# Constants out of the PSUM bank of the states, a conversion with one hand-over, normalization spread over each phase, and weights spilled in order of use

## The chip, the cores and the metric

One core of a Trainium2 chip runs the whole program. The metric is the device time of one execution in microseconds; lower is better. The engines are named as the profile names them: PE is TensorE (matmuls), PEld its weight loads, DVE VectorE, ACT ScalarE, POOL GpSimd, SP the queue that issues most DMAs.

## The reference

Three layers follow one another. Batch is 4, the sequence 768, the model width 384 (8 heads of 48).

```python
# 1. gated linear attention, per head, state 48x48, y goes on as x (4, 768, 384)
state = alpha[:, :, t, :, None] * state + einsum('bhd,bhe->bhde', k[:, :, t], v[:, :, t])
y[:, :, t] = einsum('bhd,bhde->bhe', q[:, :, t], state)
# 2. gated MLP
h = gelu_tanh(x @ w_in)                    # w_in 384 x 1024
u, v = h[..., :512], h[..., 512:]
v_n = (v - mean(v)) / sqrt(var(v) + 1e-6) * g_ln
v_s = einsum('ts,bsd->btd', w_sg, v_n) + b_sg[None, :, None]   # w_sg 768 x 768
x = x + (u * v_s) @ w_out                  # w_out 512 x 384
# 3. Fourier mixing and channel MLP
u = x + real(fft(fft(x, axis=1), axis=2))
out = u + relu(layernorm(u) @ w_ch1) @ w_ch2                   # 384 x 1536 x 384
```

## The kernel before

All three layers are in one program and overlap only at their seams; each engine executes its instructions in the order in which the code writes them. Precise products are made of three matmuls on a high and a low part (`mm3`, L425 to L427).

**Attention.** The 32 heads are taken as 16 groups of two heads; a group `g` is done in two "halves" `h` of three 128-column chunks each. One pass of the loop over `h` writes: for the group two ahead, on even halves `scan1` (L105, a scan along the sequence, then a tiny maximum and a reciprocal) and on odd halves `khat` (L118), `scan2` (L114) and, on POOL, `qhat` (L127); on even halves also `zscan` (L150), which sums the state contributions; then the scores `sc` of half `h+1` and their masking `att` (L163, tile `at`); two `fill` calls, which hand out one step each of the weight conversion below; `pv` (L171 to L177), and `kv` of the next group (L145, L146). `kv` writes the 288 columns of `kp`, a view of a whole PSUM bank `full`. In the same bank lie four constants, one column each: `one` and `tiny`, which the scans and the maximum read, and two bit masks, which the conversion reads. So whoever reads a constant and whoever writes `kp` are ordered one behind the other.

**Weight conversion.** The weights come as 64-bit floats and are put together as 32-bit floats by class `Wide`, in 62 jobs of 128 rows by 256 or 192 columns: 12 for `win` (w_in), 8 for `wo` (w_out) and 42 "spill" jobs for w_ch1 and w_ch2, which go back to DRAM for the last layer. A job takes two steps. `first`: a bit mask on DVE (L444 with the mask in PSUM, in the attention; L442 with an immediate, afterwards), then three ACT instructions (`mid`, `low`, and a relu on `x`). `second`: a sum on POOL (L464), an or on DVE (L465), a second bit mask on DVE (L444 or L442), then on POOL a product (L467) and a sum (L468). A job then ends with a split into high and low parts (ACT, and POOL L399) or with a DMA. The `fill` calls of the attention take steps until the 12 `win` jobs and 6 spill jobs are done: 19 jobs have both steps behind them by half 20, one in each half from half 2.

**Gated MLP** (`gmlp`). Per batch row `b` there are six `v` units and eight `u` units (matmuls and a gelu each, `vunit` and `uunit`), the normalization `norm(b)` of `v` (13 tiny DVE instructions, then for each of six tiles L684 and, on DVE after a copy on ACT, L687 into `vl`), and `spatial(b)`: 8 rounds `d` of 18 matmuls with `vl`, `vh` and `wsg`, a gating chain on DVE and ACT, and the output product `wout` with `wo`. The row order is: early units, the last eight of `us(1)`, `spatial(0)`, `vs(2) + us(2)` (14 units), `spatial(1)`, `vs(3)` (6 units), `spatial(2)`, `us(3)` (8 units), `spatial(3)` together with the Fourier mixing. `proj` runs a phase of units and hands out the normalization for the spatial stage that follows, one step a unit, two in the last `n` units, and what is left behind the last unit. `gfill` hands out conversion steps, `3 + d % 2` a round in `spatial` and `c` a unit in `proj`.

The scan is listed in the order of instructions below as SCALAR_TENSOR_TENSOR and in the profile as TENSOR_TENSOR_SCAN.

## Time and profile before

| what | value |
|---|---|
| median of 3 runs | 830.95 us (826.39, 830.95, 830.97) |
| profiled execution, its own time | 830.67 us |
| its span in the profile | 828.9 us |
| mean granted clock of PE, share of full speed | 0.951 |
| PE, PEld busy | 766.2 us (92%), 707.7 us (85%) |
| DVE, ACT, POOL busy | 509.8 us (61%), 321.3 us (39%), 260.7 us (31%) |

The span is cut by the work on PE: attention 0 to 205.5 us, `us(1)` to 218.0, `spatial(0)` to 273, `vs(2) + us(2)` to 305, `spatial(1)` to 345.7, `vs(3)` to 359.5, `spatial(2)` to 404.4, `us(3)` to 418.5, `spatial(3)` with the mixing to 477, and the channel MLP to the end. The share of busy time is a mean over these stages; a stage is read by which engine has no gaps in it, and by what ended the gaps of the others. The profile's view of the chain that ended last is empty here, so the reading goes by stretches, waits and timelines. In a timeline row the bracket is the time that the engine sat idle before the instruction, and what released it.

### The profile page before, as it was taken

What the parts mean: (1) busy time and instruction counts of PE and PEld (TensorE: products, weight loads), DVE (VectorE), ACT (ScalarE), POOL (GpSimd) and SP (SyncE); (2) the same over time, 40 slices, a digit from 0 to 9 for tenths busy, and PEclk for the clock granted to TensorE, in tenths of its full rate; (3) what the DMA queues carried; (4) which work ended last, traced back from release to release, by engine and by line L of the source; (5) the groups of instructions that cost most, each with busy time, mean ns of one, the idle gap of its engine ahead of it and who ended that gap; (6) DMA issues with size and microseconds to landing.
All of it is one profiled execution on the core that took longest, in us unless ns stands there. A gap on an engine that the chain in (4) does not pass through costs nothing.

```text
span 828.9 us, 13575 instructions
## 1 busy us (share of the span) xinstructions
PE 766.2 (92%) x5077; PEld 707.7 (85%) x5077; DVE 509.8 (61%) x1166; ACT 321.3 (39%) x757; POOL 260.7 (31%) x309
## 2 busy tenths in 40 slices
PE   7688888999779979879999999999999999999996
PEld 5476667777769779859999989999999999999996
DVE  6787688774578888896657767336643354424321
ACT  3555656653554464442233345123222222122210
POOL 2366765430467666634023276102000000000000
PEclk9755898999989999989999999999999999999999
DMA  9978576723412333320012033000000000000001
GB/s 231 195 172 167 125 163 159 169 59 75 122 52 77 105 93 98 90 62 30 1 42 77 1 87 105 29 1 29 2 29 2 30 1 1 30 1 28 11 19 33
DMA packets 43596, 58.07 MB, mean 70 GB/s; under 512 B 5472, under 2 KB 34176, under 8 KB 43520
## 3 DMA queue, kind: packets, MB, share of 16 engines
q1 hardware_dynamic: 42944, 56.85, 27.2%
q8 instruction: 42, 0.69, 0.3%
q10 hardware_dynamic: 576, 0.26, 0.1%
q14 instruction: 34, 0.28, 0.1%
HBM read 42.93 MB, written 9.44 MB: 63 GB/s over the span
## 4 chain that ended last, share of the span: by engine, by line


## 5 line engine op out<-in xcount | busy, mean ns | idle before, releaser
L1031 DVE SCALAR_TENSOR_TENSOR hl<-h,hh 128x384 fp32r<-128x384 f32 x96 | 53.4, 556 | 143.4 <-ACT hh L1030 143.4
L1030 ACT ACTIVATE hh<-h 128x384 fp32r<-128x384 f32 x96 | 47.2, 492 | 178.0 <-PE h L427 178.0
L425 PE MATMUL h<-unh,wc 128*128 128x384 f32 x288 | 99.3, 345 | 0.0
L426 PE MATMUL h<-unl,wc 128*128 128x384 f32 x288 | 96.5, 335 | 0.1
L427 PE MATMUL a<-wc,hl 128*128 128x384 f32 x288 | 96.4, 335 | 0.0
L427 PE MATMUL h<-unh,wc 128*128 128x384 f32 x288 | 96.3, 334 | 0.0
L426 PE MATMUL a<-wc,hh 128*128 128x384 f32 x288 | 96.2, 334 | 0.0
L425 PE MATMUL a<-wc,hh 128*128 128x384 f32 x288 | 96.2, 334 | 0.0
L427 PE MATMUL h<-wsg,vl 128*128 128x384 f32 x192 | 67.3, 351 | 5.8 <-DVE vl L687 5.8
L426 PE MATMUL h<-wsg,vh 128*128 128x384 f32 x192 | 67.3, 351 | 4.4 <-POOL wsg L399 4.4
L425 PE MATMUL h<-wsg,vh 128*128 128x384 f32 x192 | 67.0, 349 | 0.0
L467 POOL TENSOR_TENSOR wm<-wm,wr 128x192 f32<-128x192 f32 (+1 forms) x62 | 45.3, 731 | 47.1 <-DVE wr L442 29.6
L426 PEld LDWEIGHTS h<-unl,wc 128*128 128x128 f32 x288 | 54.2, 188 | 0.3 <-DVE unl L399 0.3
L427 PEld LDWEIGHTS a<-wc,hl 128*128 128x128 f32 x288 | 54.1, 188 | 0.2 <-DVE hl L1031 0.2
L425 PEld LDWEIGHTS h<-unh,wc 128*128 128x128 f32 x288 | 54.1, 188 | 0.0
L425 PEld LDWEIGHTS a<-wc,hh 128*128 128x128 f32 x288 | 54.1, 188 | 0.0
L427 PEld LDWEIGHTS h<-unh,wc 128*128 128x128 f32 x288 | 54.1, 188 | 0.0
L426 PEld LDWEIGHTS a<-wc,hh 128*128 128x128 f32 x288 | 54.1, 188 | 0.0
L464 POOL TENSOR_TENSOR wm<-wm,wr 128x192 f32<-128x192 f32 (+1 forms) x62 | 47.1, 759 | 20.8 <-ACT wr L459 20.6
L468 POOL TENSOR_TENSOR wm<-wx,wm 128x192 f32<-128x192 f32 (+1 forms) x62 | 48.6, 784 | 4.9
L465 DVE SCALAR_TENSOR_TENSOR wx<-wr,wx 128x192 int32<-128x192 int32 (+1 forms) x62 | 29.2, 472 | 29.3 <-ACT wx L460 29.3
L460 ACT ACTIVATE wx<-wx,bias 128x192 int32<-128x192 int32 (+1 forms) x62 | 29.8, 480 | 43.1 <-DVE wx L442 27.4
(217 smaller groups left out, 1951.5 us busy)
## 6 DMA issues: line engine op xcount, KB each, us to landing
ak<-in_qa SPq DMA_DIRECT2D x26, 290.4 KB, 4.8
v<-in_v SPq DMA_DIRECT2D x16, 288.0 KB, 4.2
wr<-in_w_d SPq DMA_DIRECT2D x18, 256.0 KB, 2.7
wr<-in_w_d SPq DMA_DIRECT2D x24, 192.0 KB, 2.4
raw<-w_s SPq DMA_DIRECT2D x12, 384.0 KB, 3.3
out<-o SPq DMA_DIRECT2D x24, 192.0 KB, 1.9
...
```

Of the source, the lines that this page charges most:

```text
L425: T.matmul(out, lh, rh, start=first, stop=False)
L426: T.matmul(out, lh, rl, start=False, stop=False)
L427: T.matmul(out, ll, rh, start=False, stop=last)
L460: nc.scalar.activation(x, x, AF.Relu, scale=8.0, bias=self.const)
L464: nc.gpsimd.tensor_tensor(out=mid, in0=mid, in1=j["low"], op=ALU.add)
L465: nc.vector.scalar_tensor_tensor(out=x, in0=hi, scalar=-2 ** 31, in1=x, op0=ALU.bitwise_and, op1=ALU.bitwise_or)
L467: nc.gpsimd.tensor_tensor(out=mid, in0=mid, in1=hi.bitcast(F32), op=ALU.mult)
L468: nc.gpsimd.tensor_tensor(out=mid, in0=x.bitcast(F32), in1=mid, op=ALU.add)
L1030: A.activation(hh, p, AF.Relu)
L1031: V.scalar_tensor_tensor(out=hl, in0=p, scalar=0.0, in1=hh.bitcast(F32), op0=ALU.max, op1=ALU.subtract)
```

## The change

- The four constants leave the PSUM bank: `kp` is a tile of its own columns, `one` an SBUF tile, `tiny` and the masks immediates. The multiplier `pb` of `zscan` becomes two fixed tiles, and ACT writes five of six columns of it.
- The conversion in the attention (`on_dve`): `first` is a bit mask on DVE (L446), the relu on ACT, and a `scalar_tensor_tensor` on DVE (L450) for `mid` and `low` together; `second` is the or (L460), the second mask (L461) and the product (L463) on DVE, and one sum on POOL (L466). After the attention the old form stays.
- The jobs run `win`, `wo`, spill, with the spill in the order in which the last layer uses it; the attention takes steps only until the 12 `win` jobs are done, 13 jobs by half 14.
- `gfill` hands out 4 steps a round instead of `3 + d % 2`. `proj` spreads the seven steps of `norm` evenly over the units. The phases around `spatial(2)` are `vs(3)` and four units of `us(3)` before it, and the other four after it.
- The pool of the conversion lies on the other side of the memory, and what is left of it is drained after `gmlp`.

```diff
-    full = ps_t.tile([128, 512], F32, name="kp")
-    bank, masks = full[0:R2], [full[:, D * NC + 2 + i:D * NC + 3 + i].bitcast(I32) for i in range(2)]
-    kp, one, tiny = bank[:, 0:D * NC].rearrange("p (e c) -> p e c", c=NC), bank[:, D * NC:D * NC + 1], bank[:, D * NC + 1:D * NC + 2]
+    kp = ps_t.tile([R2, D, NC], F32, name="kp")
+    one = const("one", [R2, 1])
+    pbs = [const(f"pb{i}", [R2, D, NC]) for i in range(2)]
...
-        V.tensor_tensor(out=p0, in0=sf[:, cs, 0], in1=tiny.to_broadcast(list(p0.shape)), op=ALU.max)
+        V.tensor_scalar(out=p0, in0=sf[:, cs, 0], scalar1=1e-14, scalar2=None, op0=ALU.max)
...
-            G[g]["pb"] = w_p.tile([R2, D, NC], F32, tag="pb", name="pb")
-            A.copy(G[g]["pb"], sfs[g % 3][:, None, :, 0].to_broadcast([R2, D, NC]))
+            A.copy(pbs[g % 2][:, :, 1:], sfs[g % 3][:, None, 1:, 0].to_broadcast([R2, D, NC - 1]))
...
-        self.mask(x, j["hi"], 0)
-        nc.scalar.activation(mid, h16[:, :, 2], AF.Copy, scale=2.0 ** -20)
-        nc.scalar.activation(low, h16[:, :, 1], AF.Copy, scale=2.0 ** -36)
-        nc.scalar.activation(x, x, AF.Relu, scale=8.0, bias=self.const)
+        nc.vector.tensor_scalar(out=x, in0=j["hi"], scalar1=0x7FFF0000, scalar2=None, op0=ALU.bitwise_and)
+        j["on_dve"] = self.on_dve
+        if self.on_dve:
+            nc.scalar.activation(x, x, AF.Relu, scale=8.0, bias=self.const)
+            nc.vector.scalar_tensor_tensor(out=mid, in0=h16[:, :, 2], scalar=65536.0, in1=h16[:, :, 1], op0=ALU.mult, op1=ALU.add)
+        else:
...
-        nc.gpsimd.tensor_tensor(out=mid, in0=mid, in1=j["low"], op=ALU.add)
+        if not j["on_dve"]:
+            nc.gpsimd.tensor_tensor(out=mid, in0=mid, in1=j["low"], op=ALU.add)
         nc.vector.scalar_tensor_tensor(out=x, in0=hi, scalar=-2 ** 31, in1=x, op0=ALU.bitwise_and, op1=ALU.bitwise_or)
-        self.mask(hi, x, 1)
-        nc.gpsimd.tensor_tensor(out=mid, in0=mid, in1=hi.bitcast(F32), op=ALU.mult)
+        nc.vector.tensor_scalar(out=hi, in0=x, scalar1=-2 ** 23, scalar2=None, op0=ALU.bitwise_and)
+        if j["on_dve"]:
+            nc.vector.scalar_tensor_tensor(out=mid, in0=mid, scalar=2.0 ** -36, in1=hi.bitcast(F32), op0=ALU.mult, op1=ALU.mult)
+        else:
+            nc.gpsimd.tensor_tensor(out=mid, in0=mid, in1=hi.bitcast(F32), op=ALU.mult)
         nc.gpsimd.tensor_tensor(out=mid, in0=x.bitcast(F32), in1=mid, op=ALU.add)
...
+    for q in range(KF // 2):
+        for i in range(KD):
+            c = slice(q * 256, q * 256 + 256)
+            js.append((rows(st["w1_d"], i, c, True), 256, put("w1_s", i, c)))
+        for i in (2 * q, 2 * q + 1):
+            for c in (slice(0, 192), slice(192, 384)):
+                js.append((rows(st["w2_d"], i, c, True), 192, put("w2_s", i, c)))
...
-    def proj(units, b, n, c):
-        ns = norm(b)
+    def proj(units, b, c):
+        ns, n = norm(b), NT + 1
...
-            take(ns, 1 + (i >= len(units) - n))
+            take(ns, n * (i + 1) // len(units) - n * i // len(units))
...
-                st["gfill"](h, 3 + d % 2)
+                st["gfill"](h, 4 if b < B - 1 else 2)
...
-    proj(vs(3), 2, 1, 1)
+    proj(vs(3) + us(3)[0:KH], 2, 1)
     spatial(2)
-    proj(us(3), 3, 0, 1)
+    proj(us(3)[KH:], 3, 0)
...
-    wide = wd.steps(first + spill[0:6] + second + spill[6:])
+    wide = wd.steps(first + second + spill)
...
-    front(lambda n, h: take(wide, n) if wd.n_done < len(first) + 6 else None, F["wsg"])
+    front(lambda n, h: take(wide, n) if wd.n_done < len(first) else None, F["wsg"])
     ready(len(first))
-    st["wo_ready"] = lambda d: ready(len(first) + 6 + len(second) * (d + 1) // KH)
+    st["wo_ready"] = lambda d: ready(len(first) + len(second) * (d + 1) // KH)
```

On DVE in the attention, from one masking of the scores to the next, this stands in a row before (`sf`, `ak`, `qh` are the tiles of the scans, `wr` the raw weights, `wx` and `wm` the parts of a job):

```order
L163 TENSOR_TENSOR at<-sp,mask 128x768
L444 TENSOR_TENSOR wx<-wr,kp 128x256
L465 SCALAR_TENSOR_TENSOR wx<-wr,wx 128x256
L444 TENSOR_TENSOR wr<-wx,kp 128x256
L150 SCALAR_TENSOR_TENSOR z<-kp,pb 112x288
L105 SCALAR_TENSOR_TENSOR sf_121<-ak_115,kp 112x779
L106 MEMSET ak_115 112x6
L108 TENSOR_TENSOR p_825<-sf_121,kp 112x6
L109 RECIPROCAL ak_115<-p_825 112x6
L163 TENSOR_TENSOR at<-sp,mask 128x768
L444 TENSOR_TENSOR wx<-wr,kp 128x256
```

And now, from the same masking:

```order
L162 TENSOR_TENSOR at<-sp,mask 128x768
L446 TENSOR_SCALAR wx<-wr 128x256
L450 SCALAR_TENSOR_TENSOR wm<-wr 128x256
L460 SCALAR_TENSOR_TENSOR wx<-wr,wx 128x256
L461 TENSOR_SCALAR wr<-wx 128x256
L463 SCALAR_TENSOR_TENSOR wm<-wm,wr 128x256
L149 SCALAR_TENSOR_TENSOR z<-kp,pb_129 112x288
L105 SCALAR_TENSOR_TENSOR sf_121<-ak_115,one 112x779
L106 MEMSET ak_115 112x6
L108 TENSOR_SCALAR p_805<-sf_121 112x6
L109 RECIPROCAL ak_115<-p_805 112x6
L162 TENSOR_TENSOR at<-sp,mask 128x768
```

Each job has five instructions on DVE in place of three, none reads `kp`, and the scan of L105 reads `one`.

On PE, at the states of one half (a name behind "waits" is the engine or queue whose semaphore is waited for), before:

```order
L172 MATMUL y<-at,v 48x128
L171 MATMUL y<-at,v 64x128
L172 MATMUL y<-at,v 48x128
L177 MATMUL y<-qh_124,z 48x128 x6
L145 MATMUL kp<-v,kt 64x48 [waits DVE_49,Activation_49]
L146 MATMUL kp<-v,kt 48x48
L145 MATMUL kp<-v,kt 64x48
L146 MATMUL kp<-v,kt 48x48
```

And now:

```order
L171 MATMUL y<-at,v 48x128
L170 MATMUL y<-at,v 64x128
L171 MATMUL y<-at,v 48x128
L176 MATMUL y<-qh_124,z 48x128 x6
L144 MATMUL kp<-v,kt 64x48 [waits Activation_49]
L145 MATMUL kp<-v,kt 48x48
L144 MATMUL kp<-v,kt 64x48
L145 MATMUL kp<-v,kt 48x48
```

The wait of the first `kp` matmul for DVE is gone; the one for ACT, which copies `kt`, stays.

On DVE at the end of the phase ahead of `spatial(2)`, where `vt` and `vl` are the tiles of the normalization and `bs` the statistics of the next row, before:

```order
L617 BN_STATS bs_92<-vt_87 128x6
L618 BN_AGGR mv_90<-bs_92 128x2
L684 TENSOR_SCALAR vt_86<-vt_86,mv_89,gy 128x512
L687 TENSOR_TENSOR vl<-vt_86,vh 128x512
L442 TENSOR_SCALAR wx<-wr 128x192
L617 BN_STATS bs_91<-vt_87 128x6
L618 BN_AGGR mv_90<-bs_91 128x2
L684 TENSOR_SCALAR vt_86<-vt_86,mv_89,gy 128x512
L687 TENSOR_TENSOR vl<-vt_86,vh 128x512 x2
L465 SCALAR_TENSOR_TENSOR wx<-wr,wx 128x192
L442 TENSOR_SCALAR wr<-wx 128x192
L617 BN_STATS bs_92<-vt_87 128x6
```

And now:

```order
L446 TENSOR_SCALAR wx<-wr 128x256
L683 TENSOR_SCALAR vt_86<-vt_86,mv_89,gy 128x512
L686 TENSOR_TENSOR vl<-vt_86,vh 128x512
L460 SCALAR_TENSOR_TENSOR wx<-wr,wx 128x256
L461 TENSOR_SCALAR wr<-wx 128x256
L683 TENSOR_SCALAR vt_86<-vt_86,mv_89,gy 128x512
L686 TENSOR_TENSOR vl<-vt_86,vh 128x512
L446 TENSOR_SCALAR wx<-wr 128x256
L686 TENSOR_TENSOR vl<-vt_86,vh 128x512
L460 SCALAR_TENSOR_TENSOR wx<-wr,wx 128x256
L461 TENSOR_SCALAR wr<-wx 128x256
```

Before, the statistics of the last `v` unit stand behind the last `vl`; now three `vl` stand behind all statistics, among the conversion steps of the four `u` units (L683 and L686 are L684 and L687 of before).

## Rows read from the trace of the kernel before

**Rows 1.** Busy time of each engine in three stretches (times in us).
```profile
core 0: us, PE busy (x) PEld busy (x) DVE busy (x) ACT busy (x) POOL busy (x), PEclk, DMA share, GB/s
33.00:111.00 78.00, 64.39 (x571) 49.49 (x572) 59.99 (x95) 46.74 (x117) 53.19 (x58) 0.68 0.75 163
150.00:200.00 50.00, 48.95 (x547) 39.54 (x546) 33.40 (x49) 27.22 (x62) 16.00 (x13) 1.00 0.41 91
360.00:404.50 44.50, 38.72 (x206) 37.24 (x205) 29.76 (x63) 13.74 (x33) 15.38 (x23) 0.92 0.10 30
```
**Rows 2.** Waits by pair of lines: total us, times, longest us.
```profile
PE kp L145 <- DVE wr L444: 7.9, 7, 2.5
DVE z L150 <- PE kp L146: 17.0, 10, 4.2
PE h L427 <- DVE vl L687: 5.8, 4, 2.0
```
**Rows 3.** Timeline of DVE, first scan of the third group: start, us, instruction, idle before.
```profile
24.95 1.78 DVE L105 TENSOR_TENSOR_SCAN sf<-ak,kp 112x779 f32<-112x779 f32 x1 [3.29 <-PE kp L146]
```
**Rows 4.** Timeline of DVE, one pair of halves with conversion work.
```profile
44.71 0.92 DVE L163 TENSOR_TENSOR at<-sp,mask 128x768 f32<-128x768 f32 x1
...
46.52 0.43 DVE L465 SCALAR_TENSOR_TENSOR wx<-wr,wx 128x256 int32<-128x256 int32 x1 [0.57 <-ACT wx L460]
46.98 0.42 DVE L444 TENSOR_TENSOR wr<-wx,kp 128x256 int32<-128x256 int32 x1
47.32 1.08 DVE L118 TENSOR_TENSOR sf<-ak,sf 112x768 f32<-112x768 f32 x1
...
54.33 0.76 DVE L150 TENSOR_TENSOR_SCAN z<-kp,pb 112x288 f32<-112x288 f32 x1 [0.84 <-PE kp L146]
55.00 1.75 DVE L105 TENSOR_TENSOR_SCAN sf<-ak,kp 112x779 f32<-112x779 f32 x1
...
57.10 0.92 DVE L163 TENSOR_TENSOR at<-sp,mask 128x768 f32<-128x768 f32 x1
```
**Rows 5.** Timeline of DVE, the masking of the scores at four points.
```profile
32.33 0.92 DVE L163 TENSOR_TENSOR at<-sp,mask 128x768 f32<-128x768 f32 x1
...
116.92 0.93 DVE L163 TENSOR_TENSOR at<-sp,mask 128x768 f32<-128x768 f32 x1
...
154.76 0.93 DVE L163 TENSOR_TENSOR at<-sp,mask 128x768 f32<-128x768 f32 x1
...
199.65 0.92 DVE L163 TENSOR_TENSOR at<-sp,mask 128x768 f32<-128x768 f32 x1
```
**Rows 6.** Timeline of DVE, one mask instruction at two points.
```profile
306.18 0.67 DVE L442 TENSOR_SCALAR wx<-wr 128x192 int32<-128x192 int32 x1
...
310.92 0.26 DVE L442 TENSOR_SCALAR wx<-wr 128x192 int32<-128x192 int32 x1
```
**Rows 7.** Timeline of POOL: a split, `qhat`, and the sum beside 306.18.
```profile
46.86 0.73 POOL L399 TENSOR_TENSOR win<-wm,win 128x256 fp32r<-128x256 f32 x1 [3.27 <-ACT win L396]
...
103.63 1.70 POOL L127 TENSOR_TENSOR qh<-q,qh 112x768 f32<-112x768 f32 x1
...
306.10 0.62 POOL L464 TENSOR_TENSOR wm<-wm,wr 128x192 f32<-128x192 f32 x1
```
**Rows 8.** Timeline of DVE, a conversion instruction beside the POOL instruction at 103.63.
```profile
104.72 2.27 DVE L465 SCALAR_TENSOR_TENSOR wx<-wr,wx 128x256 int32<-128x256 int32 x1 [0.57 <-ACT wx L460]
```
**Rows 9.** Timeline of PE, a wait in `spatial(0)` and one in the 14-unit phase.
```profile
233.86 0.44 PE L425 MATMUL a<-gh,wo 128*128 128x384 f32 x1 [2.20 <-ACT wo L396]
...
292.20 0.44 PE L425 MATMUL h<-xh,win 128*128 128x384 f32 x1 [1.88 <-ACT vt L614]
```
**Rows 10.** Timeline of DVE in `spatial(1)`: first of four conversion steps, and the work behind them.
```profile
326.30 0.25 DVE L442 TENSOR_SCALAR wx<-wr 128x192 int32<-128x192 int32 x1
...
329.37 0.60 DVE L719 SCALAR_TENSOR_TENSOR t<-h,gt,bb 128x384 f32<-128x384 f32 x1
```
**Rows 11.** Timeline of DVE, the last `vl` before `spatial(2)` and before `spatial(3)`.
```profile
368.40 0.68 DVE L687 TENSOR_TENSOR vl<-vt,vh 128x512 fp32r<-128x512 f32 x1
...
416.58 0.69 DVE L687 TENSOR_TENSOR vl<-vt,vh 128x512 fp32r<-128x512 f32 x1 [0.87 <-ACT vh L685]
```

More of the change, by code (lines that the diff above doesn't have):

```diff
@@ L149, in zscan @@
         z = G[g]["z"] = w_p.tile([R2, D, NC], F32, tag="z", name="z")
-        V.tensor_tensor_scan(out=flat(z), data0=flat(kp), data1=flat(G[g]["pb"]), initial=0.0, op0=ALU.add, op1=ALU.mult)
+        V.tensor_tensor_scan(out=flat(z), data0=flat(kp), data1=flat(pbs[g % 2]), initial=0.0, op0=ALU.add, op1=ALU.mult)
     def sc(h, i):
@@ L220, in attention @@
     V.memset(one, 1.0)
-    V.memset(tiny, 1e-14)
-    for m, z in zip(masks, Wide.MASKS):
-        V.memset(m, z)
-    st["wide"].masks = masks
+    for p in pbs:
+        V.memset(p[:, :, 0], 0.0)
     warmup(4)
@@ L304, in attention @@
             flag(tc, st, ones[:, 0:2], w_p, ps_t)
-    st["wide"].masks = None
+    st["wide"].on_dve = False
     ctx.close()
@@ L430 @@
 class Wide:
-    MASKS = 0x7FFF0000, -2 ** 23
     def __init__(self, nc, pool, w, const, ahead):
         self.nc, self.pool, self.w, self.const, self.ahead = nc, pool, w, const, ahead
-        self.n_done, self.masks = 0, None
+        self.n_done, self.on_dve = 0, True
     def tile(self, n, dt, w, bufs):
         return self.pool.tile([128, self.w], dt, tag=n, name=n, bufs=bufs)[:, 0:w]
-    def mask(self, out, x, i):
-        if self.masks is None:
-            self.nc.vector.tensor_scalar(out=out, in0=x, scalar1=self.MASKS[i], scalar2=None, op0=ALU.bitwise_and)
-        else:
-            self.nc.vector.tensor_tensor(out=out, in0=x, in1=self.masks[i].to_broadcast(list(x.shape)), op=ALU.bitwise_and)
     def load(self, job):
@@ L456, in first @@
         low = j["low"] = j["raw"].bitcast(F32).rearrange("p (a b) -> p a b", b=2)[:, :, 0]
[L457 to L460 removed]
+        nc.vector.tensor_scalar(out=x, in0=j["hi"], scalar1=0x7FFF0000, scalar2=None, op0=ALU.bitwise_and)
[4 more added lines that the diff above has]
+        else:
+            nc.scalar.activation(mid, h16[:, :, 2], AF.Copy, scale=2.0 ** -20)
+            nc.scalar.activation(low, h16[:, :, 1], AF.Copy, scale=2.0 ** -36)
+            nc.scalar.activation(x, x, AF.Relu, scale=8.0, bias=self.const)
     def second(self, j):
         nc, x, mid, hi = self.nc, j["x"], j["mid"], j["hi"]
[L464 removed]
+        if not j["on_dve"]:
+            nc.gpsimd.tensor_tensor(out=mid, in0=mid, in1=j["low"], op=ALU.add)
         nc.vector.scalar_tensor_tensor(out=x, in0=hi, scalar=-2 ** 31, in1=x, op0=ALU.bitwise_and, op1=ALU.bitwise_or)
[L466 to L467 removed]
+        nc.vector.tensor_scalar(out=hi, in0=x, scalar1=-2 ** 23, scalar2=None, op0=ALU.bitwise_and)
[3 more added lines that the diff above has]
+            nc.gpsimd.tensor_tensor(out=mid, in0=mid, in1=hi.bitcast(F32), op=ALU.mult)
         nc.gpsimd.tensor_tensor(out=mid, in0=x.bitcast(F32), in1=mid, op=ALU.add)
@@ L551, in spill_jobs @@
     js = []
-    for n, d, rr, cc in (("w1_s", "w1_d", KD, FF), ("w2_s", "w2_d", KF, DM)):
-        for i in range(rr):
-            w = WJ if cc % WJ == 0 else 192
-            for c in range(0, cc, w):
-                c = slice(c, c + w)
-                js.append((rows(st[d], i, c, True), w, put(n, i, c)))
+    for q in range(KF // 2):
[5 more added lines that the diff above has]
+                js.append((rows(st["w2_d"], i, c, True), 192, put("w2_s", i, c)))
     return js
@@ L695, in proj @@
                 flush()
-            take(ns, 1 + (i >= len(units) - n))
+            take(ns, n * (i + 1) // len(units) - n * i // len(units))
             st["gfill"](-1, c)
         pj.flush()
-        for _ in ns:
-            pass
     def vs(b):
@@ L752, in gmlp @@
         pass
-    proj(us(1), 0, 0, 0)
+    proj(us(1), 0, 0)
     st["after_u"](0)
@@ L756, in gmlp @@
     spatial(0)
[L757 removed]
+    proj(vs(2) + us(2), 1, 1)
     spatial(1)
[L759 removed]
+    proj(vs(3) + us(3)[0:KH], 2, 1)
     spatial(2)
[L761 removed]
+    proj(us(3)[KH:], 3, 0)
     st["after_u"](B - 1)
@@ L1113, in network @@
     st["xl"] = w1l.tile([128, NT, KD, CH], F32R, name="xl")
-    wd = Wide(nc, pool(in_u, "wide", "left"), WJ, st["bias"], 2)
+    wd = Wide(nc, pool(wts, "wide", "right"), WJ, st["bias"], 2)
     F = {}
@@ L1145, in after_u @@
             return
-        for _ in wide:
-            pass
         in_u.close()
@@ L1157, in gfill @@
     def gfill(h, n):
-        if "steps" in F:
-            return
         if h == -1:
@@ L1173, in fft @@
         if k == KH:
+            ready(len(first) + len(second) + 14)
             take(F["w2"], 2)
@@ L1185, in network @@
     gmlp(tc, st)
+    for _ in wide:
+        pass
     wts.close()
```

1 line of the change is left out of this document (removed).

## The prediction

> **What bounds the kernel now.** The table of slices says that PE is busy 92% of the span, so I first asked where it is not. The windows give it [rows 1]: from 33 to 111 us PE has 64.39 of 78 us at a granted clock of 0.68 (so mostly at its lower level of 1.2 GHz, where a matmul takes longer and looks busier), with DVE at 59.99 and POOL at 53.19. From 150 to 200 us, where no conversion is left, PE has 48.95 of 50 us at full clock. In `spatial(2)` PE has 38.72 of 44.5. The last 350 us, the channel MLP, are PE's and aren't touched.
>
> Then the waits [rows 2]. The two that the change names are there: the states' matmuls wait 7.9 us in all for the conversion's masks, and `zscan` waits 17.0 us for the states. The timeline tells what they cost. In the pair of halves of [rows 4] the second mask (46.98) reads the bank of `kp`; later `zscan` at 54.33 sat idle 0.84 us for the states. DVE is otherwise full: a pair takes 57.10 − 44.71 = 12.39 us, and its idle time is for the relu of ACT (0.57 us in these rows, and once more in the pair) and for the states (0.84). DVE and the hand-overs around it bound this stage; halves 2 and 15 begin at 32.33 and 116.92 [rows 5], 84.59 us for 13 halves, 6.5 each. Without conversion a half takes (199.65 − 154.76) / 9 = 4.99 us [rows 5], and there PE bounds it.
>
> **The change, part by part.**
>
> Start. The scan at 24.95 waited 3.29 us for the states only because `one` lies in their bank [rows 3]. It now reads SBUF; behind it comes `zscan`, which does need the states, so the scan moves ahead by up to its own 1.78 us and a little of the wait. I take −2.1, bounds −3.3 and 0.
>
> The attention without conversion. The conversion there ends with half 14 in place of half 20. Halves 15 to 20 took 154.76 − 116.92 = 37.84 us; at 4.99 they take 29.9. That is −7.9; PE needs some halves at the lower clock first, so I take −7.5, bounds −8 and −5.
>
> The attention with conversion, 13 halves. Counted on DVE, one pair has: two `at` of 0.92, `khat` 1.08, `scan1` 1.75, `scan2` (one column more) put at 1.78, `zscan` 0.76, the small ones behind `scan1` 57.10 − 55.00 − 1.75 = 0.35, and per job two bit masks and three instructions like the or of 0.43 [rows 3, 4]. A mask on 192 columns takes 0.26 undisturbed [rows 6]; I scale it to 0.28 for 256. A job is 2 × 0.28 + 3 × 0.43 = 1.85, a pair 1.84 + 1.08 + 3.53 + 0.76 + 0.35 + 3.70 = 11.26. The waits for the states and most of the relu waits go (the new instruction stands between mask and or). So if nothing else comes, −1.13 a pair, times 6.5 pairs: −7.3.
>
> But the new instructions run into POOL. The trace shows that DVE and POOL hold each other up when both read SBUF: the same mask takes 0.26 alone and 0.67 when POOL's sum at 306.10 is running [rows 6, 7]; and an or of 0.43 takes 2.27 at 104.72, when POOL began `qhat` of 1.70 at 103.63 and went on with others [rows 7, 8]. The masks (L444) and scans of before, with one operand in PSUM, show no such stretching (0.42 in [rows 4], right behind the start of a split at 46.86 in [rows 7]; scans 1.75 and 1.78). After the change the masks, the three other instructions and both scans take all operands from SBUF. The Trainium skill says why that is against the change ("SBUF — State Buffer", section "Who interferes with whom"): a DVE instruction with two SBUF inputs, or one in a two-port mode, shares a port pair with GpSimd, and whoever issues first holds it. The rows on the mask and the or agree; no row shows a scan with both inputs in SBUF. By the page the scans contend too, which is the +8 below; with free scans the same walk gives some +5.
>
> The price, from the rows: per pair DVE now has 2 × 1.85 + 1.08 + 3.53 = 8.3 us of such instructions and POOL, with one sum a job, two sums and two splits at 0.73 each and `qhat` 1.70 [rows 7], 4.6. If they exclude each other, 12.9 us are the least, when POOL is always in the shadow of `at` and `zscan`; walked through by hand (a mask behind `qhat`, two masks behind a split, a scan behind a sum, each +0.6 to 0.85) it is 13.6 to 14.1. Against 12.39 that is +0.5 to +1.7 a pair. I take +1.2, times 6.5: +8, since the measured 2.27 us shows that the waits aren't always short. Halves 11 to 14 also carry statistics and splits of `x`; they have the same excess. Bounds −7.3 (no exclusion) and +11.
>
> Attention in all: −2.1 − 7.5 + 8 = −1.6.
>
> `spatial(0)`. `wo` was behind PE: a wait of 2.20 us at 233.86 [rows 9], and another like it. `gfill` gives half a step more a round; the jobs left when the stage starts are the same 7 of `wo`. −1.5, bounds −4 and +1.
>
> The 14 units. PE waited 1.88 us at 292.20 for ACT [rows 9], the first of three such, because ACT waited with the normalization's copies for DVE. Spread over 14 units these come later, but then the last `vl` is late. −2, bounds −4 and +1.
>
> `spatial(1)`. DVE is full there: it is behind PE in every round. Four steps take 329.37 − 326.30 = 3.07 us [rows 10], 0.77 a step; four rounds of eight have one step more: +3.0, bounds 0 and +3.1.
>
> `spatial(2)`. PE waits 5.8 us for `vl` [rows 2], up to the end of the normalization: its last `vl` but one starts at 368.40 [rows 11], 9 us behind the start of the stage. The clock falls behind that (0.92 over the stage, [rows 1]), which costs (1 − 0.92) × 44.5 = 3.6 us at most. Now four `u` units stand ahead of the stage, which are 7.0 of the 14.0 us of eight, and conversion steps with them; the normalization has seven steps in ten units instead of six. DVE gets some 7 us, of which four conversion steps of 0.77 are taken; the last `vl` are still late by some 3 us. −4.4, bounds −9 and −1.
>
> `spatial(3)`. Its normalization had 14 us, and the last `vl` started at 416.58, 2 us ahead of the stage [rows 11]; it now has four units, 7.0 us, for thirteen tiny instructions and six pairs of a scaling and a `vl` of 0.69, some 1.2 each. The last `vl` come 1 to 2 us late: +1.5, bounds 0 and +4.
>
> The spill order, the other side of the memory, `pb` and the drain: 0. The conversion has 49 jobs left instead of 43, twelve steps more, and what of them costs is in the terms above. It ends before `spatial(3)`; if it didn't, its last steps would lie in a stage in which DVE has room.
>
> Gated MLP in all: −1.5 − 2 + 3.0 − 4.4 + 1.5 = −3.4. The sum is −5.0 against the profiled execution's 830.67, or 825.7; the median of the runs (830.95) is 0.3 above that, which I leave out. Measured differences within 1% (822.6 to 839.3) can't be told from no change.
>
> **Rivals.**
>
> A. No exclusion: scans and conversion aren't held up, and the waits for the states just go. For it: POOL has less to do (4.6 us a pair; a sum and a product less a job), and its instructions can fall beside `at` and `zscan`; the scans' second operand is a single element. Against it: [rows 6 to 8]. Price: −7.3 in place of +8, and a higher clock of PE can't give more, since DVE is at 11.26. 825.7 − 15.3 = 810.
>
> B. Exclusion at its worst: in every half one DVE instruction waits behind a run of POOL, as at 104.72 (2.27 − 0.43 = 1.84 us), and a second behind one more sum (0.6). A pair is 11.26 + 2 × 2.44 = 16.1 us, +3.75 against 12.39, times 6.5: +24 where I have +8. 842, slower than before. It decides from the point at which a half loses more than (8 + 5.0) / 13 = 1.0 us against before. For it: split, sum and `qhat` follow each other on POOL without a gap. Against it: there is one `qhat` in two halves, and POOL is busy only 4.6 of 12 us.
>
> C. The attention comes out as forecast, and the spread of the normalization gives what it can: `spatial(2)` −9, the 14 units −4, `spatial(0)` −4, `spatial(1)` 0: 830.7 − 1.6 − 17 + 1.5 = 814. For it: half the lost time of `spatial(2)` is the lower clock, which would not fall. Against it: DVE is full through `spatial(1)`, so it comes late into the next phase. Half of its excess over the forecast would give 820.
>
> **How the numbers follow.** The forecast, with most of its bounds (819 to 834: its terms don't all err to one side), has 0.50, A 0.26, B 0.09, C 0.15. The predicted time is 826. The range takes A's 810 with 2 us for its own spread, and leaves most of B out: 808 to 837. Faster by over 1%, below 822.6: A 0.25, C 0.11 and the lower end of the forecast 0.08, so 0.44; slower by over 1%: B's upper part and a little of the forecast's, 0.08; 0.48 within 1%.
>
> **What would show it.** Scan 1 of the third group starts at about 22 us. Scans and masks in halves 2 to 14: if some scans stay near 1.75 and others are at 2.4 or more, the exclusion is real; all at 1.75 is A. Half 15 begins at 113 to 125 us: 123 by the forecast, 108 by A, 139 by B. From there on some 5 us a half. The first `L427` of `spatial(2)` wait 3 us or less in all for `vl`, and its clock is above 0.92; `spatial(3)` has a wait for `vl` that wasn't there. The forecast is wrong if the states' matmuls still wait for DVE, if PE's clock stays low after half 14, or if the conversion reaches into `spatial(3)`.

## The result, and the profile after

The changed kernel takes 835.23 us in the median of 10 runs (834.15 to 836.5), the kernel before 826.77 on the same chip: a ratio of 1.0084, interval 1.0061 to 1.0106. It is slower by some 0.8%. The time lies in the predicted range (808 to 837); the sign and the predicted time of 826 are wrong.

One thing has to be said ahead of the stages: the runs of the kernel before fall at about 826 and at about 831 us, and both of its profiles (the one shown, and one taken again below) are of executions at 831. A comparison by stages is against that, so it shows 4.8 us where the medians differ by 8.5.

The stages, cut at PE's first instruction of each, in us of the span (828.9 and 833.7):

| stage | before | after | change | predicted |
|---|---|---|---|---|
| attention | 205.4 | 202.0 | −3.4 | −1.6 |
| `us(1)` | 12.6 | 12.6 | 0 | 0 |
| `spatial(0)` | 54.9 | 57.7 | +2.8 | −1.5 |
| 14 units | 32.2 | 26.5 | −5.7 | −2 |
| `spatial(1)` | 40.4 | 50.0 | +9.6 | +3.0 |
| `vs(3)` (after: and half of `us(3)`), `spatial(2)`, `us(3)` (or its half) | 73.0 | 73.4 | +0.4 | −4.4 |
| `spatial(3)` | 58.5 | 59.4 | +0.9 | +1.5 |
| channel MLP | 351.9 | 352.1 | +0.2 | 0 |

The attention gained more than forecast; everything behind it, −3.4 by the forecast, lost 8.2. Line numbers are now up to four lower. The first places to look at are those of [rows 5], the masking of the scores at the start of halves 2, 15 and 21:

```profile
33.15 0.92 DVE L162 TENSOR_TENSOR at<-sp,mask 128x768 f32<-128x768 f32 x1
...
124.66 0.93 DVE L162 TENSOR_TENSOR at<-sp,mask 128x768 f32<-128x768 f32 x1
...
150.91 0.93 DVE L162 TENSOR_TENSOR at<-sp,mask 128x768 f32<-128x768 f32 x1
```

The start is 0.8 us late in place of 2.1 early, but it moves by as much between profiles of the same code: the kernel before, taken again, has this masking at 33.11 (32.33 in the first profile). Halves 2 to 14 took 124.66 − 33.15 = 91.5 us, 6.9 more than before, and the six halves behind them 26.25, 11.6 less.

This cut is on DVE, which masks the scores some us before PE reads them. The attention ends on PE, so the same halves have to be cut there too, at PE's last products of halves 1, 14 and 20; before:

```profile
22.61 1.52 PE L177 MATMUL y<-qh,z 48*48 48x128 f32 x12
...
113.64 0.68 PE L177 MATMUL y<-qh,z 48*48 48x128 f32 x8
...
150.65 0.68 PE L177 MATMUL y<-qh,z 48*48 48x128 f32 x8
```

And now:

```profile
24.19 1.51 PE L176 MATMUL y<-qh,z 48*48 48x128 f32 x12
...
118.20 0.68 PE L176 MATMUL y<-qh,z 48*48 48x128 f32 x8
...
148.23 0.68 PE L176 MATMUL y<-qh,z 48*48 48x128 f32 x8
```

From the end of one row to the end of the next, PE took 90.2 us for halves 2 to 14 before and 93.2 now (+3.0), and 37.0 and 30.0 us for halves 15 to 20 (−7.0). PE lost less than DVE because part of DVE's loss used up its lead: before, PE's products of half 16 began 6.2 us behind the end of their masking (the row at 116.92 in [rows 5]), now 2.7 (the one at 124.66). By half 22 the lead is 5.2 us again (4.8 before), and that is why halves 15 to 20 look so short on DVE.

The windows that answer to [rows 1], with one of `spatial(1)` in place of the one from 150 us:

```profile
33.00:111.00 78.00, 62.74 (x565) 47.43 (x565) 73.98 (x108) 34.89 (x86) 35.06 (x32) 0.65 0.65 144
298.70:348.80 50.10, 40.77 (x210) 37.41 (x209) 41.66 (x82) 24.63 (x65) 34.56 (x46) 0.97 0.38 108
370.10:414.40 44.30, 39.76 (x208) 38.60 (x209) 29.56 (x58) 14.57 (x37) 18.51 (x26) 0.92 0.15 44
```

From 33 to 111 us DVE is now busy 73.98 of 78 us (59.99 before): in that stretch DVE hardly has a gap. In `spatial(1)` PE has work for 40.77 of 50.1 us. In the waits, the one of `kp` for the masks (7.9 us in [rows 2]) is gone, and the one for `vl`, 5.8 us there and all in `spatial(2)`, is longer in all, not shorter: 4.5 us in `spatial(2)`, 2.8 in `spatial(0)` and 1.7 in `spatial(1)`:

```profile
PE h L424 <- DVE vl L686: 9.2, 10, 2.1
```

The exclusion of DVE and POOL shows in the timelines, DVE first and POOL second, at the same stretch:

```profile
50.31 2.31 DVE L114 TENSOR_TENSOR_SCAN qh<-ak,one 112x780 f32<-112x780 f32 x1
...
53.39 1.18 DVE L446 TENSOR_SCALAR wx<-wr 128x256 int32<-128x256 int32 x1
...
55.61 0.76 DVE L461 TENSOR_SCALAR wr<-wx 128x256 int32<-128x256 int32 x1
```

```profile
49.61 1.37 POOL L466 TENSOR_TENSOR wm<-wx,wm 128x256 f32<-128x256 f32 x1 [0.69 <-DVE wm L463]
...
52.75 1.67 POOL L127 TENSOR_TENSOR qh<-q,qh 112x768 f32<-112x768 f32 x1 [1.77 <-DVE qh L114]
...
55.49 0.73 POOL L396 TENSOR_TENSOR win<-wm,win 128x256 fp32r<-128x256 f32 x1 [1.06 <-ACT win L393]
```

`scan2` at 50.31 takes 2.31 us: POOL's sum, which began at 49.61 and itself took 1.37, behind `khat`, was still running for 0.67 us. In the means from 33 to 111 us, before and now, `scan2` takes 1.77 and 2.35 us:

```profile
L114 DVE TENSOR_TENSOR_SCAN qh<-ak,kp 112x780 f32<-112x780 f32 x6 | 10.6, 1772 | 0.6 <-POOL wm L467 0.6
```

```profile
L114 DVE TENSOR_TENSOR_SCAN qh<-ak,one 112x780 f32<-112x780 f32 x6 | 14.1, 2353 | 0.0
```

Scan by scan the cause is plain. Of the 28 full scans (779 or 780 columns) of the changed kernel, the 13 that began while a POOL instruction was running took 1.85 to 2.59 us, the more the longer POOL still ran, and the other 15 took 1.75 to 1.78. Of the 28 of before, with one operand in PSUM, 20 began beside a running POOL instruction, and all took 1.75 to 1.78.

The first mask takes 1.18 behind `qhat` (52.75), the second 0.76 behind a split (55.49); alone a mask on 256 columns takes 0.28, as a run below shows.

In `spatial(1)`, a whole round on DVE, from its first to its next gating instruction (the rounds of before with four steps, 323.39 to 329.37, took some 6 us; two of its rows are [rows 10]):

```profile
323.54 0.60 DVE L716 SCALAR_TENSOR_TENSOR t<-h,gt,bb 128x384 f32<-128x384 f32 x1
324.18 0.56 DVE L717 TENSOR_TENSOR t<-t,ut 128x384 f32<-128x384 f32 x1
324.65 1.10 DVE L743 TENSOR_TENSOR xl<-x,xh 128x384 fp32r<-128x384 f32 x1
325.68 1.08 DVE L723 TENSOR_TENSOR gl<-t,gh 128x384 fp32r<-128x384 f32 x1
326.69 0.83 DVE L446 TENSOR_SCALAR wx<-wr 128x256 int32<-128x256 int32 x1
...
330.09 0.72 DVE L461 TENSOR_SCALAR wr<-wx 128x256 int32<-128x256 int32 x1
330.72 0.61 DVE L716 SCALAR_TENSOR_TENSOR t<-h,gt,bb 128x384 f32<-128x384 f32 x1
```

7.18 us, with four steps on 256 columns. It is the longest round but the next, which has another sum in it: the others take 5.9 to 6.2 us, and those with four steps on 192 columns (5.88 and 5.95) no more than before (5.7 to 6.0). Of before, all jobs in this stage had 192 columns, and every other round had three steps. Six rounds from gating to gating took 38.8 us (305.34 to 344.18) where they took 32.5 (308.47 to 340.99). In the fifth of them PE waits for the sum that DVE owes it, 2.93 us at once (1.72 before):

```profile
334.55 0.42 PE L422 MATMUL a<-gh,wo 128*128 128x384 f32 x1 [2.93 <-DVE x L737]
```

### The profile page after: what moved, and what is told of

Read it like the earlier page. It is cut to its first block, busy times and chain, and to the rows that moved or that the text cites. A ratio compares the mean times of both kernels' runs of the same rounds, so it can differ in the third digit from the quotient of the medians.

```text
span 833.7 us, 13571 instructions
## 1 busy us (share of the span) xinstructions
PE 767.9 (92%) x5077; PEld 704.6 (85%) x5077; DVE 538.9 (65%) x1191; ACT 311.2 (37%) x731; POOL 246.0 (30%) x283
## 4 chain that ended last, share of the span: by engine, by line
## 5 line engine op out<-in xcount | busy, mean ns | idle before, releaser
L422 PE MATMUL h<-wsg,vh 128*128 128x384 f32 x192 | 68.3, 356 | 1.2 <-ACT vh L684 0.7
L423 PE MATMUL h<-wsg,vh 128*128 128x384 f32 x192 | 67.7, 353 | 0.0
L466 POOL TENSOR_TENSOR wm<-wx,wm 128x192 f32<-128x192 f32 (+1 forms) x62 | 51.1, 824 | 14.9 <-DVE wm L463 10.3
L423 PEld LDWEIGHTS h<-unl,wc 128*128 128x128 f32 x288 | 54.2, 188 | 0.3 <-DVE unl L396 0.3
L422 PEld LDWEIGHTS h<-unh,wc 128*128 128x128 f32 x288 | 54.1, 188 | 0.0
L424 PEld LDWEIGHTS h<-unh,wc 128*128 128x128 f32 x288 | 54.1, 188 | 0.0
L422 PEld LDWEIGHTS a<-wc,hh 128*128 128x128 f32 x288 | 54.1, 188 | 0.0
L423 PEld LDWEIGHTS a<-wc,hh 128*128 128x128 f32 x288 | 54.1, 188 | 0.0
L127 POOL TENSOR_TENSOR qh<-q,qh 112x768 f32<-112x768 f32 (+1 forms) x18 | 29.8, 1656 | 68.2 <-DVE qh L114 53.9
L424 PEld LDWEIGHTS h<-wsg,vl 128*128 128x128 f32 x192 | 38.4, 200 | 13.4 <-DVE vl L686 13.4
L465 POOL TENSOR_TENSOR wm<-wm,wr 128x192 f32<-128x192 f32 (+1 forms) x49 | 35.1, 717 | 36.2 <-DVE wr L461 34.4
L422 PE MATMUL a<-gh,wo 128*128 128x384 f32 x96 | 33.7, 351 | 13.0 <-ACT wo L393 6.4
```

Source lines behind the costliest of these rows:

```text
L127: P.tensor_tensor(out=qh, in0=chunks(G[g]["q"])[:, cs], in1=qh, op=ALU.mult)
L422: T.matmul(out, lh, rh, start=first, stop=False)
L423: T.matmul(out, lh, rl, start=False, stop=False)
L424: T.matmul(out, ll, rh, start=False, stop=last)
L465: nc.gpsimd.tensor_tensor(out=mid, in0=mid, in1=hi.bitcast(F32), op=ALU.mult)
L466: nc.gpsimd.tensor_tensor(out=mid, in0=x.bitcast(F32), in1=mid, op=ALU.add)
```

## The experiments

Each was timed beside the kernel before on the same chip. "Parts" are the three of which the change is made: the attention (constants, `pb`, conversion), the shares of the conversion (fewer jobs in the attention, four steps a round, order of the spill, pool) and the normalization (its spread, and the phases around `spatial(2)`).

### One part at a time

The attention's part alone, on the kernel before:

```diff
-    kp, one, tiny = bank[:, 0:D * NC].rearrange("p (e c) -> p e c", c=NC), bank[:, D * NC:D * NC + 1], bank[:, D * NC + 1:D * NC + 2]
+    kp = ps_t.tile([R2, D, NC], F32, name="kp")
+    one = const("one", [R2, 1])
...
+        if self.on_dve:
+            nc.scalar.activation(x, x, AF.Relu, scale=8.0, bias=self.const)
+            nc.vector.scalar_tensor_tensor(out=mid, in0=h16[:, :, 2], scalar=65536.0, in1=h16[:, :, 1], op0=ALU.mult, op1=ALU.add)
```

> The kernel before with the attention part of the change alone (constants out of the bank, pb, the conversion with five DVE instructions), still with 18 jobs' worth of conversion in the attention. Theory 1 (DVE and POOL exclude each other, a half with conversion takes 7.05 us in place of 6.5, as in the profile of the changed kernel): 19 such halves and the start give +9 to +11 us against the kernel before. Rival (the excess belongs to halves 11 to 14 with their other work, and the waits taken away pay for the rest): within 3 us of the kernel before.

834.98 us, ratio 1.0072 (1.0043 to 1.0100). The attention took 210.6 us in the profile, +5.2, of which halves 2 to 14 were +7; the stages behind it were within 0.5 us of before, each. It is a loss, half of theory 1's size. Cut on PE, halves 2 to 14 took 92.2 us (+2.0) and halves 15 to 20, still with conversion here, 40.6 (+3.6): PE sees less than DVE loses until DVE's lead is used up. Behind half 20 PE took 54.1 us, as before (54.2).

The normalization's part alone:

```diff
-            take(ns, 1 + (i >= len(units) - n))
+            take(ns, n * (i + 1) // len(units) - n * i // len(units))
...
-    proj(vs(3), 2, 1, 1)
+    proj(vs(3) + us(3)[0:KH], 2, 1)
```

> The kernel before with the spread of the normalization and the new split of the phases around spatial(2) alone. Theory 1 (the loss in the gated MLP is conversion work moved into stages that DVE bounds): -3 to 0 us; the 14 units lose their 5 us of waits, and spatial(0) and spatial(1) start some 3 us late each. Theory 2 (the loss in the gated MLP is the normalization that ends behind the phase): +4 to +8 us, most of the +8.3 us that the changed kernel loses behind the attention.

828.25 us, ratio 0.999 (0.997 to 1.001): no change. The 14 units fell from 32.2 to 27.3 us and `spatial(1)` rose from 40.4 to 44.1, `spatial(0)` by 0.7, `spatial(3)` by 0.9; `vs(3)` to `us(3)` gained 1.3. So theory 2, the late normalization of the text above, falls as the cause of the loss: what the spread gives to the units it takes from the spatial stage behind them. In `spatial(1)` PE waited 2.3 us for `vl`, and its granted clock was 0.96 where it was 1.00. The waits for `vl` didn't shrink in all:

```profile
PE h L427 <- DVE vl L687: 8.3, 9, 1.9
```

The shares alone:

```diff
-                st["gfill"](h, 3 + d % 2)
+                st["gfill"](h, 4 if b < B - 1 else 2)
...
-    wide = wd.steps(first + spill[0:6] + second + spill[6:])
+    wide = wd.steps(first + second + spill)
...
-    front(lambda n, h: take(wide, n) if wd.n_done < len(first) + 6 else None, F["wsg"])
+    front(lambda n, h: take(wide, n) if wd.n_done < len(first) else None, F["wsg"])
```

> The kernel before with the shares of the conversion alone: 13 jobs in the attention in place of 19, four steps a round, the new order of the spill, the pool on the other side. Theory 1 (moved work): the attention gains 8 to 11 us, the gated MLP loses 6 to 9, most of it in spatial(1): -4 to +1 us in all. Theory 2 (late normalization): the attention gains the same and the gated MLP loses 3 at most, -8 to -5 us.

835.11 us, ratio 1.0072 (1.0044 to 1.0099): a loss, more than theory 1 (moved work) gave. The attention gained 7.2 us (198.2), and the gated MLP lost 12: `spatial(0)` +1.6, `spatial(1)` +6.6 (47.0), `spatial(2)` +4.3 (49.3), where DVE comes out of `spatial(1)` late and the normalization after it. The windows of these two stages:

```profile
299.00:346.00 47.00, 40.35 (x209) 37.44 (x208) 37.84 (x75) 22.92 (x61) 32.94 (x45) 0.96 0.39 113
360.00:409.30 49.30, 42.92 (x208) 39.48 (x208) 35.85 (x77) 18.25 (x44) 22.49 (x32) 0.86 0.17 49
```

The parts don't add up: +4.9, −1.5 and +5.2 us of span by themselves, +4.8 together. The rounds of `spatial(1)` do: six took 38.9 us here, as in the changed kernel. With the shares, the normalization's part is worth more than without them: the four units that stand ahead of `spatial(2)` give DVE the time to catch up there (`vs(3)` to `us(3)` 73.4 us in place of 14.0 + 49.3 + 14.1 = 77.4).

The kernel before once more:

> The kernel before, unchanged, for a second profile: its executions lie at 826 or at 831 us, and the profile shown is one at 831. If the two are told apart by the clock in the attention, the stage times from 205 us on agree within 1 us and those before differ by 4 to 5; if by the gated MLP, the other way round.

831.38 us. The profile lies at 831 again, and the stages agree within 0.6 us with the first. It doesn't tell what makes the difference to 826, and this stays open; the mean granted clock was 0.969 here and 0.951 in the first, at the same time, so it isn't the clock alone.

### Where the shares cost, and what the attention's part costs in the fastest setting

The changed kernel, with fewer steps where DVE is full and more where it isn't. The profile of the changed kernel has POOL's last conversion sum at 395.70, so most of `spatial(2)` (370.1 to 414.4) had no conversion, and DVE 29.56 of 44.3 us there:

```diff
-                st["gfill"](h, 4 if b < B - 1 else 2)
+                st["gfill"](h, (4, 2, 4, 2)[b])
```

> The changed kernel with other shares of the conversion in the gated MLP: 4, 2, 4, 2 steps a round in spatial(0) to spatial(3) in place of 4, 4, 4, 2. The conversion then ends at the end of spatial(2) and not in its fifth round. Moved work: spatial(1), bounded by DVE, loses 16 steps of 0.77 us until PE bounds it and falls from 50.1 to some 43 us, spatial(2) grows by 1 at most: 828 to 830 us. Late normalization: spatial(1) falls by 3 us at most: 832 us or more.

826.29 us, ratio 0.9977 (0.9956 to 0.9998), 9 us below the changed kernel. `spatial(1)` fell from 50.0 to 38.9 us, `spatial(2)` rose by 2.6, `spatial(0)` and `spatial(3)` by some 1 each, and the phase between `spatial(1)` and `spatial(2)` fell by 1.2. The window of `spatial(1)` shows PE as its bound again, at full clock:

```profile
298.30:337.20 38.90, 37.05 (x209) 35.90 (x208) 33.32 (x64) 17.48 (x45) 21.93 (x29) 1.00 0.30 87
```

So the loss in the gated MLP was the conversion in `spatial(1)`, as theory 1 has it, and it can be put where it costs little. The late normalization, which theory 2 took for the whole, can't explain 11 us.

The same shares and the same normalization, with the attention of before:

```diff
-        self.n_done, self.on_dve = 0, True
+        self.n_done, self.masks = 0, None
```

(and all other lines of the attention's part as before.)

> The kernel before with the shares of the conversion, the spread of the normalization, the split of the phases and 4, 2, 4, 2 steps a round, but with the attention's constants and conversion of before. If the attention's part of the change is a loss of 3 to 5 us by itself and the others add up: 3 to 5 us below the run with the same shares in the changed kernel, 823 to 826 us, which is faster than before by 0 to 0.5%. If the parts don't add up (the attention hands its lead on to a stage that waits for something else): the same time as that run.

821.0 us, ratio 0.9912 (0.988 to 0.9945): 5.3 below the run above. The attention took 195.8 us, 4.9 less, and the stages behind it differ by 1.2 us at most. The attention's part of the change is a loss by itself.

### What makes the attention's part slow

The attention's part alone as above, but with the conversion on three engines, so that only the constants change:

```diff
-        self.n_done, self.on_dve = 0, True
+        self.n_done, self.on_dve = 0, False
```

> The kernel before with the constants out of the bank alone: the scans read one from SBUF, the masks are immediates on SBUF operands, pb as in the change; the conversion keeps its three DVE and three POOL instructions in the attention, and the jobs stay where they were. If the exclusion between DVE and POOL is what the operands in SBUF cost, scans and masks now meet a POOL that is busy 7.5 us a pair of halves: halves 2 to 14 take 6.8 to 7.2 us in place of 6.5, and the whole is 5 to 10 us slower than before. Rival (the five DVE instructions are what costs): halves of 6.2 to 6.5, since the waits for the states are gone, and -4 to +1 us.

837.29 us, ratio 1.0112 (1.0078 to 1.0146); halves 2 to 14 took 94.9 us, 7.3 each. In the same window, `zscan` waited 3.8 us for the states in place of 7.5 before, and the operands in SBUF cost more than that:

```profile
L114 DVE TENSOR_TENSOR_SCAN qh<-ak,one 112x780 f32<-112x780 f32 x6 | 13.9, 2311 | 0.0
...
L118 DVE TENSOR_TENSOR sf<-ak,sf 112x768 f32<-112x768 f32 x6 | 8.4, 1406 | 0.0
...
L446 DVE TENSOR_SCALAR wx<-wr 128x256 int32<-128x256 int32 x11 | 8.7, 791 | 0.0
...
L149 DVE TENSOR_TENSOR_SCAN z<-kp,pb 112x288 f32<-112x288 f32 x5 | 3.7, 746 | 3.8 <-PE kp L145 3.8
```

`scan2` takes 2.31 us in the mean, `khat` 1.41, the first mask 0.79 where it took 0.41 on PSUM. The rival, that the five DVE instructions are what costs, falls: with two DVE instructions a job more and two on POOL less, the run with the whole part is 4 us faster than this one in the attention (210.6 to 214.7).

`qhat` on DVE, with the changed kernel's attention:

```diff
-        P.tensor_tensor(out=qh, in0=chunks(G[g]["q"])[:, cs], in1=qh, op=ALU.mult)
+        V.tensor_tensor(out=qh, in0=chunks(G[g]["q"])[:, cs], in1=qh, op=ALU.mult)
```

> As the changed kernel with 4, 2, 4, 2 steps a round, and qhat on DVE in place of POOL. Exclusion: a pair of halves gains the 1.70 us for which POOL held the port and pays 0.95 on DVE; scan2 and the masks behind qhat go back to 1.77 and 0.28 us; halves 2 to 14 take 6.6 us in place of 7.05: 4 to 6 us below the run without it. Rival (DVE is simply fuller, and the long scans have another cause): 0.95 us more a pair, 5 to 8 us above it.

826.49 us, as without it (826.29); halves 2 to 14 took 93.6 us in place of 91.5. Neither side was right: the first mask, the one behind `qhat`, goes back to its undisturbed length, but `scan2` stays long. `qhat` reads what `scan2` writes and so never ran beside the `scan2` of its group; what holds `scan2` up in both kernels is POOL's sum, which began 0.71 us ahead of it (five of the six scans in the row; the sixth met a split):

```profile
L114 DVE TENSOR_TENSOR_SCAN qh<-ak,one 112x780 f32<-112x780 f32 x6 | 14.1, 2356 | 0.0
...
L461 DVE TENSOR_SCALAR wr<-wx 128x256 int32<-128x256 int32 x11 | 7.8, 713 | 0.4
...
L446 DVE TENSOR_SCALAR wx<-wr 128x256 int32<-128x256 int32 x11 | 3.1, 282 | 0.0
```

Now the five instructions with `one` and `tiny` in the bank, and the masks in the bank or immediate (both on the run with 821.0 us; in the second, `mask` takes its immediate form everywhere):

```diff
-        self.mask(x, j["hi"], 0)
-        nc.scalar.activation(mid, h16[:, :, 2], AF.Copy, scale=2.0 ** -20)
+        self.mask(x, j["hi"], 0)
+        j["on_dve"] = self.masks is not None
+        if j["on_dve"]:
+            nc.scalar.activation(x, x, AF.Relu, scale=8.0, bias=self.const)
+            nc.vector.scalar_tensor_tensor(out=mid, in0=h16[:, :, 2], scalar=65536.0, in1=h16[:, :, 1], op0=ALU.mult, op1=ALU.add)
```

> The same base, with the conversion of five DVE instructions in the attention, but one, tiny and the masks left in the PSUM bank of kp. If the operands in SBUF are what makes scans and masks long: scans at 1.75 to 1.78 us and masks at 0.42, a pair of halves has 11.26 + 4 x 0.14 = 11.8 us of DVE work and 0.5 of waits, 6.15 a half in place of 6.4: the attention 3 to 4 us shorter than the 195.8 of the base, 817 to 818 us. Rival (the five instructions in SBUF run into POOL's split, sum and qhat by themselves): 6.4 us or more a half, the same time or up to 4 us more.

> As the run with the masks in the bank, but the masks are immediates on SBUF operands; one and tiny stay in the bank. It differs from the changed kernel's attention by the scans' operand alone. If the scans' second SBUF operand is the larger part of the excess: scans at 1.78, masks stretched (0.6 to 0.8 in the mean), 6.3 to 6.5 us a half, the attention within 2 us of the base. Rival (the masks are the larger part): 6.8 to 7.0 us a half, 4 to 6 us above the base, like the changed kernel's.

With the masks in the bank 820.39 us, ratio 0.9889 (0.9853 to 0.9926), attention 195.0; immediate 821.98 us, ratio 0.9909 (0.9875 to 0.9942), attention 196.3; the base had 821.0, 0.9912 and 195.8. These times don't tell the three apart, so the reading goes by the rows. The scans are back at 1.77 in both, and the masks tell the two apart; first the run with masks in the bank, then with immediates:

```profile
L114 DVE TENSOR_TENSOR_SCAN qh<-ak,kp 112x780 f32<-112x780 f32 x6 | 10.6, 1766 | 0.0
...
L461 DVE SCALAR_TENSOR_TENSOR wm<-wr 128x256 f32<-128x256 uint16 x12 | 8.2, 685 | 0.0
...
L444 DVE TENSOR_TENSOR wx<-wr,kp 128x256 int32<-128x256 int32 x12 | 4.9, 407 | 0.0
```

```profile
L114 DVE TENSOR_TENSOR_SCAN qh<-ak,kp 112x780 f32<-112x780 f32 x6 | 10.6, 1770 | 0.0
...
L442 DVE TENSOR_SCALAR wr<-wx 128x256 int32<-128x256 int32 x12 | 8.6, 716 | 0.4
...
L442 DVE TENSOR_SCALAR wx<-wr 128x256 int32<-128x256 int32 x12 | 7.7, 641 | 0.0
```

L461 is here the instruction for `mid` and `low`, L450 of the changed kernel. On DVE the 13 halves give a ladder: 82.8 us with all constants in the bank, 85.6 with the masks out of it (+2.8), 91.5 with `one` (and `tiny`, and the fixed `pb`) out of it as well (+5.9, the run with 826.29 us). The same attention code took 82.7 and 84.6 us in two profiles (the base and a run below), so steps under 2 us say nothing, and +2.8 is little more. By the means in the rows both masks are longer by 0.53 us together (0.64 and 0.72 against 0.41 and 0.42) and L461 shorter by 0.20, which makes +4.3 in 13 halves. On PE, over halves 2 to 20 (in which DVE wins back its lead), the ladder is 117.6, 118.4 and 123.3 us, so the masks are worth no more than the spread between profiles there, and the scans' operand 5.0. It is the larger part on both engines. What the five DVE instructions are worth as such isn't settled: on PE the base took 118.6 us for these halves and 120.4 in the later run with the same attention code, against 117.6. One of the five, L461, takes waits for POOL (0.69 in the mean, 0.42 alone). The expectation of 6.15 us a half for the bank was too low (6.37).

### A faster version

The run with 821.0 us, with the normalization of the first phase and the shares in `spatial(0)` as before:

```diff
-            take(ns, n * (i + 1) // len(units) - n * i // len(units))
+            take(ns, 1 if b == 0 else n * (i + 1) // len(units) - n * i // len(units))
...
-                st["gfill"](h, (4, 2, 4, 2)[b])
+                st["gfill"](h, (3 + d % 2, 2, 4, 2)[b])
```

> The run with the attention of before, the other parts of the change and 4, 2, 4, 2 steps a round, with two things of before put back ahead of and in spatial(0): one step of the normalization with each unit from the first on, and 3 or 4 steps a round in place of 4. If spatial(0) is 2.5 us longer than before because its normalization ends later and a half step more a round falls on DVE: spatial(0) goes from 57.4 to 55 to 56 us, and 819 to 820 us in all. Rival (spatial(0) waits for its output weights, one job after the other, whatever the share): 57 us and the same time.

818.09 us, ratio 0.9863 (0.9825 to 0.9902). `spatial(0)` went from 57.4 to 52.5 us, more than expected, and PE doesn't wait for `vl` there any more, but for `wsg` as before (3.8 us in place of 4.4); `spatial(1)` is 37.8. The run doesn't tell the two edits apart.

> The fastest run so far (first phase and spatial(0) as before, 818.1 us) with the conversion of five DVE instructions in the attention and all constants in the bank. In the run with that conversion alone the attention was 0.8 us shorter than with three instructions: 816.5 to 818 us if the two add up; 818 to 820 if the start of spatial(0) takes back what the attention gains, since it waits for a conversion of its own (wsg, wo).

816.5 us, ratio 0.9834 (0.9807 to 0.9861): the attention took 194.8 us in place of 197.9, `spatial(0)` 53.3 in place of 52.5; the two add up, as far as differences of this size can be told. It is 1.7% faster than the kernel before and 18.7 us below the changed one, which wasn't timed beside it (by the ratios, 0.9834 against 1.0084). It keeps of the change the 13 jobs in the attention, the order of the spill, the spread of the normalization in the later phases and the five instructions; it doesn't keep the constants in SBUF and the four steps a round in `spatial(1)`.

## Why the prediction was wrong

**Attention, −1.6 predicted, −3.4 measured.** The main term was right in cause: the shift onto operands in SBUF holds scans and masks up, shown by the runs above. In size it was right for DVE (+8 forecast for halves 2 to 14, +6.9 measured), but not for the time: on PE the same halves took 3.0 us more, since DVE had a lead to lose, and the sum had no term for it. The rule of the Trainium skill that was weighed there ("SBUF — State Buffer", "Who interferes with whom"), that the one that issues first keeps the other waiting, holds for the scans too, of which no row before told. The traces agree: 1.77 us with one operand in PSUM, 2.31 to 2.36 in the mean for `scan2` with both in SBUF and POOL busy, 1.75 for a scan that began ahead of `qhat` (at 29.76). Rival A, without exclusion, falls; B, a wait of 2.44 us in every half, was too dear. The term for the free halves was right, −7.5 against −7.0 on PE, 5.0 us a half; the 4.4 us a half on DVE are its lead won back. With the attention of before and the same jobs, PE took 29.8 us for them. Behind half 20 PE took 1.0 us less, with the attention of before and the same jobs too. The gain at the start, −2.1, isn't to be seen: PE ended half 1 at 25.7 where it ended it at 24.1, but other profiles have it at 23.0 to 25.3 with the attention of before and at 23.9 and 24.3 with the changed one, so no difference can be told. So −3.4 in all is near −1.6 partly by luck: the exclusion was taken 5 us too dear, and the start didn't come. `scan1` did start earlier, at 23.15 where it started at 24.95, but `zscan` behind it still waited for the states, and the next group's tiny maximum, now also on SBUF operands, met `qhat` and took 1.44 us for six columns:

```profile
23.15 1.77 DVE L105 TENSOR_TENSOR_SCAN sf<-ak,one 112x779 f32<-112x779 f32 x1
...
26.54 0.76 DVE L149 TENSOR_TENSOR_SCAN z<-kp,pb 112x288 f32<-112x288 f32 x1 [1.19 <-PE kp L145]
...
31.56 1.44 DVE L108 TENSOR_SCALAR p<-sf 112x6 f32<-112x6 f32 x1
```

**Gated MLP, −3.4 predicted, +8.0 measured.** This is where the sign was lost. The step that failed is "`spatial(1)`. DVE is full there ... four rounds of eight have one step more: +3.0". The stage took 9.6 us more. The mechanism was right and its size wrong, twice. The steps were priced at 0.77 us from a round with jobs of 192 columns, and the new order of the spill brings jobs of 256 into this stage (a round with four such steps took 7.18 us, rounds with none 5.88 and 5.95); the shares alone made +6.6 of it. How much of that is the width and how much the number of steps wasn't run apart. And the last `vl`, which the spread puts behind the 14 units, makes the stage start late: +3.7 with the normalization alone. I had put that into the term of the 14 units ("−2 ... but then the last `vl` is late") where the units themselves gained 5.7 and the stage paid the price. Rival C, in which the spread gives what it can, falls with the same run (ratio 0.999).

The step on `spatial(2)` (−4.4, measured +0.4 from `vs(3)` to `us(3)`) failed for the same reason: DVE comes out of `spatial(1)` later than before, so the four `u` units are used up by catching up. PE waited 4.5 us for `vl` in the stage (5.8 before, 3 forecast), at the same clock of 0.92. Once `spatial(1)` had two steps a round, this wait fell to 1.3 us, and `vs(3)` to `us(3)` took 74.8 us with the conversion in it.

The step on `spatial(0)` (−1.5, measured +2.8): the waits for `wo` stayed, three of 1.9 us and 6.4 in all (4.4 before), and waits for `vl` came to it at the start (2.8), where those for `wsg` of before (4.4) went. In all PE waited 12.1 us in place of 11.2; the rest of the +2.8 isn't explained. That the jobs of `wo` left at that point were the same was right, but not the conclusion that PE waits less.

`spatial(3)` was near the forecast (+0.9 against +1.5), but PE hardly waited there for `vl` (0.3 us), which was the reason given. The stages that hide conversion at little cost were named in the prediction ("if it didn't, its last steps would lie in a stage in which DVE has room") but not used: the question that the sum should have asked is not only how many steps come to the gated MLP, but whether they come to a stage that PE bounds or to one that DVE bounds.
